# Rows of the batch-end store ordered by batch first instead of by token first

## Chip, cores and metric

The kernel runs on one core of a Trainium2 chip. The metric is device time in microseconds (us), the median of several executions. The span of a profile is some 1.8 us shorter than the time of the same execution.

## The reference

Attention with sliding-window masks (plain for four heads, dilated for four), then a mixture of experts with soft slots. Only the shape of the result matters here: 8 batches of 576 tokens give 4608 rows of 512 float32 numbers, 9.4 MB in all.

In outline (shortened, not the code itself):

```python
def reference(q, k, v, moe_phi, moe_w1, moe_w2):
    x = attention(q, k, v)                  # 8 batches x 576 tokens -> (4608, 512)
    logits = x @ phi                        # 32 slots
    slot_out = experts(softmax(logits, 0).T @ x, w1, w2)
    return softmax(logits, 1) @ slot_out    # (4608, 512), float32
```

## The kernel before

The last stage multiplies the exponentials of the logits (tile `o_et`, one column for each token) by the slot outputs, scales the rows while it evicts them from PSUM (the memory that takes TensorE's results), and stores them. It works in groups of 512 tokens: 128 partitions, each with four consecutive rows, so 8 KB that are contiguous in SBUF and in DRAM. 576 is not a multiple of 512. Groups 0 to 7 are the first 512 tokens of each batch; group 8 collects the last 64 tokens of all eight batches. Its exponentials are first copied together on GpSimd, and it is written by the batch-end store, whose 128 runs of 8 KB lie in eight places in DRAM, 576 rows apart.

```python
    def tok(G, j):                                  # weights of one output matmul
        return (a(o_et + 576 * G + j, [[4, 128]]) if G < 8 else
                a(o_tail + j, [[4, 128]]))
    # ... cut ...
    op(POOL, lambda: pool.tensor_copy(              # the tail copy
        a(o_tail, [[4, 8], [32, 16], [1, 4]]), a(o_et + 512, [[576, 8], [4, 16], [1, 4]])), ...)
    # ... cut ...
    def store(G, c0, cw, prio, j0=0, n=4):
        if G < 8:
            dst = out[576 * G:576 * G + 512, c0:c0 + cw].rearrange("(p j) f -> p j f", j=4)[:, j0:j0 + n, :]
            src = af(ostg(G) + 2 * (512 * j0 + c0), [[512, n], [1, cw]])
        else:                                       # the batch-end store: partition 8i+b
            dst = out.rearrange("(b r) f -> b r f", b=8)[:, 512:576, :].rearrange("b (i j) f -> i b (j f)", j=4)
            src = af(ostg(G), [[1, 2048]])
        store_ops.append(op(SP, lambda: spq.dma_start(dst, src), ...))
    # ... cut: ten stores of 256 KB, one of 512 KB, and then six of 1 MB, in this order:
    for G, x in [(2, 2)] + [(G, x) for G in (8, 3, 4, 5, 6, 7) for x in (0, 2)]:
```

The softmax here doesn't subtract the row's maximum and nothing guards it: scores larger than these inputs give would overflow.

## Time and profile before

| | before |
|---|---|
| time, median | 180.82 us |
| span of the profile | 179.0 us |
| last instruction of a compute engine ends | 164.5 us |
| rest of the span, stores draining | 14.5 us |

The chain of waits of before, its last pieces. The columns are start, length, and what.

```profile
120.53 32.06 DMA ar<-in_moe_w_dram
...
153.89 8.63 DVE ar L913 x15
...
163.18 1.32 DVE ar L913 x2
```

Up to 152.6 us the kernel waits for expert weights, then it evicts output tiles (L913) until 163.18 + 1.32 = 164.5 us. The chain as the profile follows it stops there. What runs on to 179.0 us is seen in the stretches. Here the columns are the stretch and its length, busy time of each engine (PE is TensorE, PEld its weight loads, DVE VectorE, ACT ScalarE, POOL GpSimd; SP, below, is the engine that issues the stores), the granted TensorE clock, the mean busy share of the 16 DMA engines, and GB/s. A packet counts whole in the stretch in which it starts, so a share can pass 1.

```profile
core 0: us, PE busy (x) PEld busy (x) DVE busy (x) ACT busy (x) POOL busy (x), PEclk, DMA share, GB/s
159.00:161.00 2.00, 1.93 (x9) 0.44 (x6) 2.00 (x4) 2.00 (x5) 0.00 (x0) 1.00 1.10 373
161.00:163.00 2.00, 1.26 (x5) 0.26 (x3) 2.00 (x4) 2.00 (x4) 0.00 (x0) 1.00 0.96 205
163.00:165.00 2.00, 0.00 (x0) 0.00 (x0) 1.50 (x3) 0.22 (x1) 0.00 (x0) 1.00 1.07 307
165.00:167.00 2.00, 0.00 (x0) 0.00 (x0) 0.00 (x0) 0.00 (x0) 0.00 (x0) 0.77 0.94 381
167.00:169.00 2.00, 0.00 (x0) 0.00 (x0) 0.00 (x0) 0.00 (x0) 0.00 (x0) 0.50 1.00 418
...
175.00:177.00 2.00, 0.00 (x0) 0.00 (x0) 0.00 (x0) 0.00 (x0) 0.00 (x0) 0.50 0.95 397
177.00:179.00 2.00, 0.00 (x0) 0.00 (x0) 0.00 (x0) 0.00 (x0) 0.00 (x0) 0.50 0.18 74
```

The DMA engines are busy without a break from before 160 us to 177 us (shares of 0.94 to 1.10): the end of the kernel is a queue of stores that drains. In the stretch from 161 to 163 us they are as busy as later (0.96 against 1.00 at 167 to 169 us) but move only half as much (205 against 418 GB/s). That is when the batch-end store runs. It was issued at 158.0 us and took 8.3 us to land, as the view of the output tensor, cut to that moment, shows:

```profile
L926 SPq DMA_DIRECT2D out_dram<-ar x1: 648/648/648, 158.0 to 158.0; - x1
...
DMA to landing us min/median/max: 8.3/8.3/8.3
```

The trace also keeps a record of every DMA packet (start, duration, bytes, queue; not the engine). Of the 768 packets of 8 KB that the six whole-tile stores make, the median takes 309 ns and 88 take more than 450 ns. Because one packet follows the other almost without a gap, packets can be strung together by their times; these are two such strings through the batch-end store of before, in ns:

```
795 596 631 558 518 645 386 606
309 572 598 818 309 309 309 684
```

### The profile page before, as it was taken

Reading aid. Unit: us, or ns where it says so; the run is one execution under the profiler, and the core shown is the slowest. Engines: PE = TensorE matmul, PEld = TensorE weight load, DVE = VectorE, ACT = ScalarE, POOL = GpSimd, SP = SyncE. Lnnn points to the kernel's source line nnn. Section 1 sums busy time; section 2 is a strip of 40 time slices with the busy share of each in tenths; the row PEclk is TensorE's granted clock in tenths of the full one; section 3 lists DMA queues with packets and bytes.
Section 4 is the critical chain, followed back from the end, with each engine's and each line's share of the span. In section 5 each row is a group of like instructions: output and inputs, shape, how many; then the busy total and the mean of one; then the engine's idle time right before and its main releaser. Section 6 shows DMA issues by size and latency. Waiting matters only on the chain.

```text
span 179.0 us, 4780 instructions
## 1 busy us (share of the span) xinstructions
PE 127.9 (71%) x2093; PEld 87.5 (49%) x2094; DVE 118.0 (66%) x220; ACT 104.7 (58%) x165; POOL 51.7 (29%) x103
## 2 busy tenths in 40 slices
PE   0009778989789989989699989976697657892000
PEld 0006556666567767767477767664444224420000
DVE  6898579788899899899589699383300015797000
ACT  2405299797789799798666889875111004694000
POOL 7559741332423432333930000790100000000000
PEclk9999999999999999999965999999879999999555
DMA  6999999999999999999999999999999999899996
GB/s 185 234 213 210 217 207 215 211 211 210 218 207 213 215 209 210 215 210 210 215 208 212 213 211 217 211 215 210 219 209 217 196 195 230 304 356 264 421 419 260
DMA packets 19220, 41.26 MB, mean 230 GB/s; under 512 B 1920, under 2 KB 8576, under 8 KB 18304
## 3 DMA queue, kind: packets, MB, share of 16 engines
q0 software_dynamic: 15056, 30.41, 90.0%
q1 hardware_dynamic: 4144, 10.55, 16.6%
q8 instruction: 16, 0.26, 0.5%
q14 instruction: 4, 0.03, 0.0%
HBM read 61.93 MB, written 9.44 MB: 399 GB/s over the span
## 4 chain that ended last, share of the span: by engine, by line
DMA 32%; PE 23%; DVE 23%; ACT 6%; POOL 4%; issue 2%; DVEq 0%
DMA ar<-in_moe_w_dram 18%; DMA ar<-in_k_dram 15%; PE ps L509 7%; DVE ar L488 6%; DVE ar L913 6%; ACT ar L548 4%; POOL ar L371 4%; PE ps L603 3%; DVE ar L614 3%; PE ps L570 3%; PE ps L516 2%; PE ps L526 2%; PE ps L693 2%; DVE ar L494 2%; DVE ar L445 2%
## 5 line engine op out<-in xcount | busy, mean ns | idle before, releaser
L548 ACT ACTIVATE ar<-ps 128x1152 bf16<-128x1152 f32 (+1 forms) x32 | 38.0, 1186 | 22.8 <-PE ps L533 12.5
L488 DVE STREAM_TRANSPOSE ar<-ar 128x576 uint32<-128x576 uint32 x40 | 48.4, 1240 | 3.1 <-DMA ar<-in_k_dram 2.9
L509 PE MATMUL ps<-ar 128*128 128x320 bf16 (+1 forms) x128 | 23.9, 313 | 15.4 <-DVE ar L488 13.1
L614 DVE TENSOR_TENSOR ar<-ps,fs 96x768 bf16<-96x768 f32 (+1 forms) x32 | 26.3, 823 | 1.2
L576 ACT ACTIVATE ar<-ps 128x768 bf16<-128x768 bf16 x32 | 24.8, 811 | 2.2 <-PE ps L570 2.2
L509 PEld LDWEIGHTS ps<-ar 128*128 128x128 bf16 x128 | 10.9, 102 | 20.1 <-POOL ar L418 13.1
L603 PE MATMUL ps<-ar 128*128 128x65 bf16 x320 | 15.7, 200 | 3.4 <-ACT ar L548 3.1
L570 PE MATMUL ps<-ar 128*128 128x128 bf16 x192 | 16.3, 232 | 2.2 <-DVE ar L614 1.9
L910 ACT ACTIVATE ar<-ps,fs 128x512 f32<-128x512 f32 (+1 forms) x23 | 11.4, 641 | 8.3 <-PE ps L901 8.3
L603 PEld LDWEIGHTS ps<-ar 128*128 128x128 bf16 x320 | 12.9, 101 | 6.3 <-ACT ar L548 3.8
L335 POOL DMA_DIRECT2D ar<-in_k_dram x16 | 8.9, 553 | 23.1 <-DVE ar L488 18.2
L610 DVE RECIPROCAL fs<-ps 96x12 f32<-96x12 f32 (+1 forms) x32 | 6.4, 200 | 12.6 <-PE ps L603 12.4
L570 PEld LDWEIGHTS ps<-ar 128*128 128x128 bf16 x192 | 12.8, 120 | 3.6 <-DVE ar L614 2.4
L857 PE MATMUL ps<-ar 128*32 128x512 bf16 (+1 forms) x80 | 10.5, 338 | 5.0 <-DMA ar<-in_moe_w_dram 3.5
L913 DVE TENSOR_SCALAR ar<-ps,fs 128x512 f32<-128x512 f32 (+1 forms) x23 | 12.7, 628 | 1.0 <-PE ps L901 1.0
L364 POOL DMA_DIRECT2D ar<-in_moe_w_dram x12 | 6.4, 580 | 22.2 <-DVE ar L488 22.2
L335 POOL DMA_DIRECT2D ar<-in_q_dram x16 | 8.7, 546 | 11.5 <-DVE fs L610 6.6
L335 POOL DMA_DIRECT2D ar<-in_v_dram x16 | 8.8, 549 | 9.2 <-DVE fs L610 5.5
L670 ACT ACTIVATE ar<-ps 128x576 bf16<-128x576 bf16 x16 | 9.6, 652 | 2.3 <-PE ps L654 2.3
L901 PE MATMUL ps<-ar 128*128 128x512 bf16 (+1 forms) x45 | 9.8, 339 | 1.5 <-DVE ar L881 1.0
L693 PE MATMUL ps<-ar 128*128 128x288 bf16 x64 | 9.2, 287 | 1.2 <-ACT ar L677 1.2
L857 PEld LDWEIGHTS ps<-ar 128*32 128x32 bf16 x80 | 4.7, 96 | 10.6 <-DMA ar<-in_moe_w_dram 6.8
(75 smaller groups left out, 192.6 us busy)
## 6 DMA issues: line engine op xcount, KB each, us to landing
ar<-in_moe_w_dram POOLq DMA_DIRECT2D x29, 512.0 KB, 27.2
out_dram<-ar SPq DMA_DIRECT2D x6, 1024.0 KB, 11.0
ar<-in_k_dram POOLq DMA_DIRECT2D x16, 288.0 KB, 21.8
ar<-in_q_dram POOLq DMA_DIRECT2D x16, 288.0 KB, 22.3
ar<-in_v_dram POOLq DMA_DIRECT2D x16, 288.0 KB, 22.3
out_dram<-ar SPq DMA_DIRECT2D x10, 256.0 KB, 3.8
ar<-in_moe_w_dram SPq DMA_DIRECT2D x1, 1024.0 KB, 4.9
ar<-in_moe_w_dram POOLq DMA_DIRECT2D x2, 256.0 KB, 31.7
```

What stands on the lines that cost most here:

```text
L335: return pool.dma_start(a(o_stg + (s * 3 + j) * 1152, [[1, 1152]]), src[b, 4 * dl:4 * dl + 4].rearrange("h (p t) d -> (h p) (t d)", p=32))
L488: return dve.transpose(au(o_dst, [[1, 18], [18, 32]]), au(src, [[32, 18], [1, 32]]))
L509: pe.matmul(pf(h, 0, [[1, W]]), a(o_id, [[1, 128]]), a(msk, [[1, W]]), start=True, stop=False)
L548: eo = op(ACT, lambda P=P, W=W: act.activation(a(P, [[W, 4], [1, W]]), AP(ps, 0, [[4096, 128], [512, 4], [1, W]]), ACTF.Exp, scale=SCALE), ...
L570: last = pe.transpose(pb(bank.idx, bb * 256 + par * 32, [[64, 4], [1, 32]]), src, a(o_id, [[1, 128]]))
L576: op(ACT, lambda t=t, bank=bank: act.activation(a(o_vb[vs] + 3 * t * VBK, [[66, 12], [2, 32], [1, 2]]), pb(bank.idx, 0, [[64, 12], [1, 32] ...
L603: last = pe.matmul(pf(bank.idx + x, 65 * t, [[1, 65]]), w, a(VB + t * VBK + 66 * h, [[1, 65]]), start=True, stop=True)
L614: op(DVE, lambda hp=hp, bank=bank: dve.tensor_tensor(a(ox + 128 * hp, [[64, 2], [256, NT], [1, 64]], 0, rows), pf(bank.idx, 0, [[512, 2], ...
L693: last = pe.matmul(pf(bank.idx, 0, [[1, 288]]), a(o_phis + 128 * c, [[1, 128]]), a(o_xt[xt] + 576 * c + 288 * g, [[1, 288]]), start=(c == ...
L857: last = pe.matmul(pf(sobank[x].idx, 0, [[1, n]], 32 * j, 32), a(o_htz + 1024 * g + 128 * c + 32 * j, [[1, 32]]), a(w2off(e) + DM * c + co ...
L910: op(ACT, lambda: act.activation(dst, src(), ACTF.Copy, scale=sca), actt(cw, .1), prio + .1, reads=[bank, b_rinv], writes=wr, name=f"OE{G} ...
L913: op(DVE, lambda: dve.tensor_scalar(dst, src(), sca, None, op0=AluOp.mult), dvet(cw, True) + .08, prio + .1, reads=[bank, b_rinv], writes= ...
```

## The change

The intent is to have the batch-end store write the 64 rows of one batch, 128 KB in one piece, from 16 neighbouring partitions, and to make the tail copy simpler. Partition 8i+b becomes partition 16b+i.

```diff
     op(POOL, lambda: pool.tensor_copy(
-        a(o_tail, [[4, 8], [32, 16], [1, 4]]), a(o_et + 512, [[576, 8], [4, 16], [1, 4]])), .8, T1 + 4, reads=[b_et],
+        a(o_tail, [[64, 8], [1, 64]]), a(o_et + 512, [[576, 8], [1, 64]])), .8, T1 + 4, reads=[b_et],
         writes=[b_tail], name="tail")
@@
-            dst = out.rearrange("(b r) f -> b r f", b=8)[:, 512:576, :].rearrange("b (i j) f -> i b (j f)", j=4)
+            dst = out.rearrange("(b r) f -> b r f", b=8)[:, 512:576, :].rearrange("b (i j) f -> b i (j f)", j=4)
```

The instruction lists of the two kernels differ in these two instructions only; the destination goes from 16x8x2048 to 8x16x2048.

## The prediction

> **What bounds the kernel now.** From 120.5 to 152.6 us the chain of waits sits on weight loads, then on output evictions (VectorE, 8.6 us). After 164.5 us no compute engine works any more; the span ends at 179.0 us: the last 14.5 us are the store queue draining. Between 167 and 177 us the DMA share is 0.95 to 1.04, at 397 to 438 GB/s (windows). The queue is behind from about 160 us on: the batch-end store is issued at 158.0 us and lands 8.3 us later, while the last of the five whole-tile stores behind it is issued at 166.1 us. So what a DMA engine loses in the batch-end store comes out at the end, one for one, on the slowest engine.
>
> **The batch-end store is already slow.** In the DMA records, 8 KB packets of the later stores take 309 ns; those of this store, between about 160.5 and 165.9 us, mostly take 550 to 650 ns (the stretch 161 to 163 us moved only 205 GB/s at 0.96 busy). [...] A rival reading is interference at the HBM end.
>
> **What the change does.** The GpSimd copy into the tail tile has the same 128x512 elements (630 ns, at 125.4 us, needed only after 152 us) and no other compute instruction changes: worth 0. The store keeps 128 runs of 8 KB, but its destination's outermost dimension goes from 16 to 8. [...] Eight engines then carry 16 packets each instead of 8, the others none; the later stores stay evenly split, so the loaded engines end last.
>
> **Cost (estimates from packet durations).** Before: eight packets at about 540 ns mean, slowest engine about 5.3 us. After: sixteen packets. Without collisions 16 x 0.309 = 4.9 us: no change. [...] 16 x 0.54 = 8.6 us: +3.3 us. [...] I expect nearly the worst of the three: 186.8 us (+3.3%), range 181.5 to 191. Chances: faster by over 2% 0.02, within 2% 0.25, slower by over 2% 0.73.
>
> **What would show it.** The store's issue to landing grows from 8.3 us to about 14 us; its packets stay at 600 to 900 ns; the drain after the last eviction grows from 14.5 to about 20 us; in the last 4 to 8 us only half of the DMA engines are busy (share near 0.5).
>
> **What would make it wrong.** If the store still spreads over 16 engines, there is no imbalance, and without collisions the time could fall by up to 2.6 us. If the present slowness comes from HBM and batch-first order cures it, doubling packets and halving their time cancel: no change. If engines drift out of step, collisions fade and the loss is 2 to 3 us, within 2%.

## The result, and the profile after

| | before | after |
|---|---|---|
| time, median | 180.85 us | 190.01 us |
| ratio, 95% interval | 1 | 1.0508 (1.0486 to 1.053) |
| span | 179.0 us | 188.0 us |
| last eviction ends | 164.5 us | 164.5 us |
| stores draining after it | 14.5 us | 23.5 us |

A ratio here is the mean time of one kernel's fast runs over that of the other's in the same rounds, so it is not quite the ratio of the medians quoted.

The evictions of after end where they did. This is the last piece of its chain of waits:

```profile
163.22 1.32 DVE ar L913 x2
```

So the whole 9 us is in the drain. Its stretches, same columns:

```profile
core 0: us, PE busy (x) PEld busy (x) DVE busy (x) ACT busy (x) POOL busy (x), PEclk, DMA share, GB/s
...
161.00:163.00 2.00, 1.30 (x5) 0.26 (x3) 2.00 (x4) 2.00 (x4) 0.00 (x0) 1.00 1.01 258
163.00:165.00 2.00, 0.00 (x0) 0.00 (x0) 1.53 (x3) 0.27 (x1) 0.00 (x0) 0.72 0.83 242
165.00:167.00 2.00, 0.00 (x0) 0.00 (x0) 0.00 (x0) 0.00 (x0) 0.00 (x0) 0.50 0.88 254
...
177.00:179.00 2.00, 0.00 (x0) 0.00 (x0) 0.00 (x0) 0.00 (x0) 0.00 (x0) 0.50 0.58 246
179.00:181.00 2.00, 0.00 (x0) 0.00 (x0) 0.00 (x0) 0.00 (x0) 0.00 (x0) 0.50 0.36 152
181.00:183.00 2.00, 0.00 (x0) 0.00 (x0) 0.00 (x0) 0.00 (x0) 0.00 (x0) 0.50 0.24 102
183.00:185.00 2.00, 0.00 (x0) 0.00 (x0) 0.00 (x0) 0.00 (x0) 0.00 (x0) 0.50 0.22 94
185.00:187.00 2.00, 0.00 (x0) 0.00 (x0) 0.00 (x0) 0.00 (x0) 0.00 (x0) 0.50 0.13 53
```

From 179 us on fewer and fewer engines work, and the last 2 us belong to 0.13 x 16 = 2 of them. An engine that works to 187 us with 40 packets of later stores (five stores, eight packets each) at 309 ns to do must have finished the batch-end store 12.4 us earlier, at about 174.6 us. This store's first packet starts at 160.5 us, so its 16 packets took about 14.1 us. This is worked out from the stretches and the packet times; the profile gives no landing time for this store. The records of 4 bytes, one from each engine at the end of each store, agree: on the two engines that end last they come 2.45 us apart, and the sixth from the end is at 174.73 and 174.92 us. So the store took these two engines 14.2 to 14.4 us, 0.89 to 0.90 us a packet on the mean.

One line of the page counts the packets of the SP queue, here of before and then of after:

```profile
q1 hardware_dynamic: 4144, 10.55, 16.6%
```

```profile
q1 hardware_dynamic: 4136, 10.55, 16.3%
```

The bytes are the same and eight packets are missing, all of 4 bytes in the records. In before there are 304 of them for the 19 transfers of this queue (17 stores and two loads), 16 to each, which fits one completion signal from each DMA engine that takes part. So the store uses eight engines now. In the records of after, 125 of the 768 packets of 8 KB take over 450 ns, and 29 take over 1000 ns (12 of them 1170 to 1190 ns, 3.8 times the 309 ns of a quiet packet); in before none takes over 1000.

The records of after show more when they are strung together. Of the eight engines that have nothing of the batch-end store, six do their first later store, eight packets, at 309 ns each and end it at 163.05 to 163.14 us. The two others take 594 to 613 ns for seven of their eight packets and end it at about 165.4 us. Four of the loaded engines take 1179 to 1184 ns for each packet that starts between 161.2 and 162.9 us, and the other four mostly about 0.6 us. Against the 309 ns of a quiet packet, then, six of the engines that have gone ahead lose nothing, two take about twice as long, and four loaded ones 3.8 times as long. What decides which is which is not in the profile: the records name neither engine nor partition, and the strings are put together by their times alone. The single execution of dst_only, below, shows the same first ends: six at 163.21 to 163.28 us, two at 165.53 and 165.68 us.

### The profile page after: what moved, and what is told of

Its sections match the earlier page's. It is cut to its first block, busy times and chain, and to the rows that moved or that the text cites. A ratio compares the mean times of both kernels' runs of the same rounds, so it can differ in the third digit from the quotient of the medians.

```text
span 188.0 us, 4781 instructions
## 1 busy us (share of the span) xinstructions
PE 125.3 (67%) x2094; PEld 84.9 (45%) x2094; DVE 117.2 (62%) x220; ACT 105.1 (56%) x165; POOL 51.7 (28%) x103
## 4 chain that ended last, share of the span: by engine, by line
DMA 57%; DVE 19%; PE 4%; POOL 4%; issue 2%; ACT 1%; DVEq 0%
DMA ar<-in_k_dram 39%; DMA ar<-in_moe_w_dram 18%; DVE ar L488 6%; DVE ar L913 5%; POOL ar L371 3%; DVE ar L614 2%; PE ps L509 1%; DVE ar L445 1%; DVE ar L450 1%; PE ps L570 1%; PE ps L516 1%; ACT ar L670 1%; ACT ar L548 1%; POOL ar L364 1%; DVE ar L494 1%
## 5 line engine op out<-in xcount | busy, mean ns | idle before, releaser
L509 PE MATMUL ps<-ar 128*128 128x320 bf16 (+1 forms) x128 | 22.8, 302 | 15.8 <-DVE ar L488 13.1
L509 PEld LDWEIGHTS ps<-ar 128*128 128x128 bf16 x128 | 10.5, 99 | 20.4 <-POOL ar L418 13.1
L603 PE MATMUL ps<-ar 128*128 128x65 bf16 x320 | 14.7, 193 | 3.3 <-ACT ar L548 3.2
L857 PE MATMUL ps<-ar 128*32 128x512 bf16 (+1 forms) x80 | 11.5, 367 | 5.7 <-DMA ar<-in_moe_w_dram 5.1
L570 PEld LDWEIGHTS ps<-ar 128*128 128x128 bf16 x192 | 12.4, 118 | 5.3 <-DVE ar L614 3.8
L603 PEld LDWEIGHTS ps<-ar 128*128 128x128 bf16 x320 | 12.0, 97 | 6.0 <-ACT ar L548 3.7
L901 PE MATMUL ps<-ar 128*128 128x512 bf16 (+1 forms) x46 | 10.8, 367 | 1.3 <-DVE ar L881 1.0
L857 PEld LDWEIGHTS ps<-ar 128*32 128x32 bf16 x80 | 5.3, 104 | 11.7 <-DMA ar<-in_moe_w_dram 8.0
```

The lines of the kernel that those rows point to most:

```text
L509: pe.matmul(pf(h, 0, [[1, W]]), a(o_id, [[1, 128]]), a(msk, [[1, W]]), start=True, stop=False)
L570: last = pe.transpose(pb(bank.idx, bb * 256 + par * 32, [[64, 4], [1, 32]]), src, a(o_id, [[1, 128]]))
L603: last = pe.matmul(pf(bank.idx + x, 65 * t, [[1, 65]]), w, a(VB + t * VBK + 66 * h, [[1, 65]]), start=True, stop=True)
L857: last = pe.matmul(pf(sobank[x].idx, 0, [[1, n]], 32 * j, 32), a(o_htz + 1024 * g + 128 * c + 32 * j, [[1, 32]]), a(w2off(e) + DM * c + co ...
```

## The experiments

Four theories stand against each other: the loss is **imbalance** (eight engines carry 16 packets each, and the rest of the queue is split evenly); it is **collisions within the store** (engines at work on it slow each other, depending on the SBUF partitions that they read); it is **meetings** (the loaded engines run into those that have gone ahead to the next stores); or it is **DRAM** (the order of addresses). Which partitions would collide was the author's assumption, and the layouts of per_batch and split4_last were chosen by it; the runs test it by packet times alone. The control per_batch_i and per_batch set collisions within the store against DRAM.

### dst_only: the store without the copy

```diff
 # before, with the new destination and the old tail copy
-    .rearrange("b (i j) f -> i b (j f)", j=4)
+    .rearrange("b (i j) f -> b i (j f)", j=4)
```

> Only the store's destination order of the change, with the old tail copy; rows are stored in the wrong place, so the result is wrong on purpose. If the whole loss is the store's, 190 us; what is missing from that is the copy's share, expected 0.

Measured: 189.58 us in one execution (before 180.92 us), its result wrong. The loss is the store's; the copy's share is at most some tenths.

### per_batch_i and per_batch: the same DRAM order from other partitions

```diff
 # batch-end store cut into eight, one for each batch bb
+            for bb in range(8):
+                d8 = out[576 * bb + 512:576 * bb + 576, :].rearrange("(i j) f -> i (j f)", j=4)
+                s8 = <16 partitions: bb, bb + 8, ... bb + 120>       # per_batch_i, with the copy of before
+                s8 = af(ostg(G), [[1, 2048]], 16 * bb, 16)           # per_batch, with the copy of after
```

> Before, with the batch-end store cut into eight stores of 16 rows of 8 KB, one for each batch; the row of each batch and block leaves from the same SBUF partition (8i+b) as before [...]. It is the control for the next run. Both theories [...] expect the same packets as before, 550 to 650 ns, and 180.8 to 182 us; the excess over 180.8 is the cost of issuing seven more stores.

> After, with the store cut into eight stores, one for each batch: 16 rows of 8 KB from the 16 neighbouring partitions 16b to 16b+15. DRAM addresses and their order by engine are the same as in the control; only the SBUF partitions differ, and all 16 engines carry eight packets again. [...] packets of about 1200 ns, the store takes about 9.9 us in place of 5.3, and the time is about 185 us, some 4.5 us over the control. DRAM theory: packets and time as in the control. Pure imbalance theory (the loss of the change comes only from eight engines carrying all): as in the control, since nothing is unbalanced.

Measured: per_batch_i 180.59 us (ratio 0.9988, 0.9973 to 1.0003), per_batch 181.46 us (1.0035, 1.0018 to 1.0053). In per_batch_i no packet takes over 788 ns; in per_batch 19 take over 1000 ns. Both send the same rows to the same DRAM addresses in the same eight stores, with 16 engines (4256 packets of the queue in both, 112 or 7 x 16 more than in before), so the long packets come with the other SBUF partitions: this speaks against DRAM. Which engine writes which row is not in the records. The expected 1200 ns and 4.5 us were the author's estimates of collisions within the store, for four engines that slow each other, which is not shown; the 4.5 us became 0.9 us. The records show why a packet's length is a poor measure of the loss (the mean over all 768 packets is 358 ns, against 342 in per_batch_i). Three strings of per_batch (ns):

```
1232 309 867 309 391
1160 309 1049 309 309
994 309 966 309 309
```

After a packet of 1.0 to 1.2 us comes one of 309 ns, so the store as a whole does not take four times as long; why is not shown. Issuing may pace this store too: the eight issues take 5.6 us on SP, about as long as the packets of this store in before (160.5 to 165.9 us). The run shows collisions, but is a poor measure of their price.

### after_last: eight engines, nobody ahead of them

```diff
-    for G, x in [(2, 2)] + [(G, x) for G in (8, 3, 4, 5, 6, 7) for x in (0, 2)]:
+    for G, x in [(2, 2)] + [(G, x) for G in (3, 4, 5, 6, 7, 8) for x in (0, 2)]:
```

> After, with the batch-end store issued last instead of first of the six whole-tile stores. The same eight engines carry 16 packets, but no later store runs beside them. If part of the 9 us comes from meeting the engines that have gone ahead [...], that part goes: [...] 16 packets at about 0.6 us = 9.6 us at the end, total about 185 us. If the loss comes from the engines' own collisions and imbalance alone, position does not matter and it stays at 190 us. In the last 8 to 10 us the DMA share should be 0.5 at some 105 GB/s.

Measured: 182.95 us (1.0116, 1.01 to 1.0133). Moving the store to the end wins back 7.1 us of the 9.2. Its last stretches:

```profile
173.00:175.00 2.00, 0.00 (x0) 0.00 (x0) 0.00 (x0) 0.00 (x0) 0.00 (x0) 0.50 0.59 127
175.00:177.00 2.00, 0.00 (x0) 0.00 (x0) 0.00 (x0) 0.00 (x0) 0.00 (x0) 0.50 0.43 123
177.00:179.00 2.00, 0.00 (x0) 0.00 (x0) 0.00 (x0) 0.00 (x0) 0.00 (x0) 0.50 0.48 188
179.00:181.00 2.00, 0.00 (x0) 0.00 (x0) 0.00 (x0) 0.00 (x0) 0.00 (x0) 0.50 0.21 90
```

Half of the engines work; at first they move 123 to 127 GB/s, then 188. A string of 16 packets says the same (ns):

```
606 629 631 565 562 625 474 316 567 321 312 312 309 309 309 309
```

Seven of the first nine packets take 562 to 631 ns, the last seven 309 to 321 ns: the collisions end within the store. That the engines start in step and then fall out of step is the author's reading and not shown. I had expected all 16 packets to stay near 0.6 us (9.6 us); the store took some 7 us (7.16 us in this string).

### split4_last: the same imbalance without collisions

The tail copy is laid out so that partition 32x+4b+i holds four rows of batch b, and the store is cut into four.

```diff
 # after_last, and:
+            for x in range(4):
+                d8 = out(batch, row, f)[:, 512 + 16 * x:528 + 16 * x, :].rearrange("b (i j) f -> b i (j f)", j=4)
+                s8 = af(ostg(G), [[1, 2048]], 32 * x, 32)          # 32 partitions for each part
```

> As after_last, but the last store is cut into four, each of 8 batches by 4 rows from 32 partitions, [...]. Still eight engines with 16 packets each, so the imbalance is that of after_last. [...] packets of 309 ns, 16 of them = 5 us at the end at some 210 GB/s, total about 180.5 us, 4 to 5 us under after_last. If collisions are not the cause, as after_last.

Measured: 180.93 us (1.0008, 0.9993 to 1.0023). The queue shows eight completion packets for each of the four stores (4160 packets in all, 16 more than before), so there are eight engines here too.

```profile
173.00:175.00 2.00, 0.00 (x0) 0.00 (x0) 0.00 (x0) 0.00 (x0) 0.00 (x0) 0.50 0.48 197
175.00:177.00 2.00, 0.00 (x0) 0.00 (x0) 0.00 (x0) 0.00 (x0) 0.00 (x0) 0.50 0.54 197
177.00:179.00 2.00, 0.00 (x0) 0.00 (x0) 0.00 (x0) 0.00 (x0) 0.00 (x0) 0.50 0.23 98
```

Half of the engines (shares of 0.48 and 0.54) move almost half of the full rate (197 GB/s against 426 at 171 to 173 us). Only 8 packets of 768 take over 450 ns, none over 596: this layout hardly collides, as the author had assumed. The imbalance is that of after_last, the place in the queue too, and the time is 2.0 us shorter: that is the price of collisions within the store. It also speaks against DRAM again, as each part is still stored by batch first.

### split4_here: the same four parts at the old place

```diff
 # split4_last, with the order of before
-    ... (3, 4, 5, 6, 7, 8) ...
+    ... (8, 3, 4, 5, 6, 7) ...
```

> The four-part batch-end store of split4_last, at its old place, ahead of the five other whole-tile stores. Eight engines carry it, they never meet one another; [...] If meeting engines that have gone ahead is what costs, this is 8 packets at 309 ns and 8 at about 618, 7.4 us, 2.5 us over split4_last: about 183 us. If imbalance alone costs nothing and meetings cost nothing, 181 us. If the place in the queue itself costs [...], near the 190 us of after.

That half of the packets would meet an engine that has gone ahead, and take twice 309 ns then, was the author's estimate; no run shows it.

Measured: 181.72 us (1.0049, 1.0032 to 1.0065), 0.8 us over split4_last where 2.5 were expected. The profile shows that the run tested less than it was to test:

```profile
161.00:163.00 2.00, 1.47 (x5) 0.26 (x3) 2.00 (x4) 2.00 (x5) 0.00 (x0) 1.00 0.50 197
163.00:165.00 2.00, 0.00 (x0) 0.00 (x0) 1.71 (x3) 0.43 (x1) 0.00 (x0) 1.00 0.72 242
165.00:167.00 2.00, 0.00 (x0) 0.00 (x0) 0.00 (x0) 0.00 (x0) 0.00 (x0) 1.00 0.94 225
```

Issuing four parts took SP until 162.45 us, and the next store had not reached the other eight engines before about 164.3 us: until then they were idle, and nobody was met. From 165 to 167 us, when both kinds are at work, 0.94 of the engines move only 225 GB/s. The place in the queue alone does not cost 9 us; the size of the meetings is left to the next run.

### after_hold: a wait added

```diff
 # after, with one dependency more
+                            after=[<the batch-end store>]   # stores behind it are issued when it has landed
```

> After, with one wait added: the store behind the batch-end store is issued only when that store has landed, so nothing runs beside its eight engines, and eight engines stand idle meanwhile. All stores, their order and their addresses are those of after. If the loss of after comes from the loaded engines meeting those that have gone ahead [...], the batch-end store now takes some 7 us, as in after_last, and with a gap of about 2 us for landing and issuing the total is about 185 us: a wait that saves some 5 us. If the meetings are not what costs, the wait can only add: 190 us or more.

Measured: 184.58 us (1.0202, 1.0187 to 1.0217). All stores, addresses and their order are those of after; SP waits 9.3 us for the store to land, eight engines are idle meanwhile, and the kernel is 5.4 us faster than after.

```profile
161.00:163.00 2.00, 1.46 (x5) 0.26 (x3) 2.00 (x4) 2.00 (x5) 0.00 (x0) 1.00 0.49 98
163.00:165.00 2.00, 0.00 (x0) 0.00 (x0) 1.70 (x3) 0.43 (x1) 0.00 (x0) 1.00 0.48 147
165.00:167.00 2.00, 0.00 (x0) 0.00 (x0) 0.00 (x0) 0.00 (x0) 0.00 (x0) 0.80 0.50 193
167.00:169.00 2.00, 0.00 (x0) 0.00 (x0) 0.00 (x0) 0.00 (x0) 0.00 (x0) 0.50 0.13 53
169.00:171.00 2.00, 0.00 (x0) 0.00 (x0) 0.00 (x0) 0.00 (x0) 0.00 (x0) 0.50 0.96 393
```

The share of 0.48 to 0.50 while this store is alone is a second sign of eight engines. No packet takes over 845 ns: the packets of 1.2 us of after came only with another store beside. The gap (0.13 at 167 to 169 us) is the price of the wait; it is the likely cause of the 1.6 us by which this run is slower than after_last, but no run separates it.

### before_last: the same move with 16 engines

```diff
 # before, with the order of after_last
-    ... (8, 3, 4, 5, 6, 7) ...
+    ... (3, 4, 5, 6, 7, 8) ...
```

> Before, with its 16-engine batch-end store issued last. Here all engines carry it at once in either place, so few meet engines that have gone ahead: 180 to 181 us, within 0.5% of before, against the 7 us that the same move was worth with eight engines (190.0 to 182.95 us). If the place in the queue itself costs, some us faster than before.

Measured: 180.13 us (0.9958, 0.9945 to 0.9971). With 16 engines the place is worth 0.4%, with eight it was worth 7.1 us.

### uniform and uniform2: no batch-end store at all

Group G takes rows 512G to 512G+511 regardless of batches. All stores are then even runs of 128 rows of 8 KB, and the tail copy goes. In uniform all row sums come from one block of 36 small matmuls at the end; in uniform2 they come with the sums of each batch.

```diff
-        return (a(o_et + 576 * G + j, [[4, 128]]) if G < 8 else a(o_tail + j, [[4, 128]]))
+        return a(o_et + 512 * G + j, [[4, 128]])
@@ store
-        dst = out[576 * G:576 * G + 512, ...   (and the batch-end case)
+        dst = out[512 * G:512 * G + 512, c0:c0 + cw].rearrange("(p j) f -> p j f", j=4)[:, j0:j0 + n, :]
@@ uniform2, in the matmuls of the sums of batch b (batch 7 also for group 8)
+            for t in range(4 * b, 4 * b + (8 if b == 7 else 4)):
+                last = pe.matmul(pf(bank.idx, 363 + t - 4 * b, [[1, 1]]), tok(t // 4, t % 4), a(o_rm, [[1, 1]]), ...)
```

> Before, with the nine output groups laid over the 4608 rows without regard to batches (group G holds rows 512G to 512G+511, the row sums and their reciprocals are taken for all groups at once in the idle time before the last weights come), so that every whole-tile store is one even run of 128 rows of 8 KB and there is no batch-end store and no tail copy. If the batch-end store of before loses some 2.6 us [...], all six stores run at 309 ns a packet from about 160.5 us on and the time is about 178.2 us (1.5% under before). If its slow packets cost nothing because something else paces the drain, it stays at 180.8.

Measured: 180.40 us (0.9975, 0.9952 to 0.9998), correct. The drain was as hoped, but it began later. The pieces of its chain of waits before the drain, and the same piece of before:

```profile
146.81 4.51 PE ps L849 x55
...
155.17 0.44 DVE ar L873
...
156.11 8.64 DVE ar L905 x15
```

```profile
152.95 0.44 DVE ar L881
```

The last sum of slot outputs (L873, L881 in before) ends 2.2 us later, in the slowest of six executions (179.85 to 181.25 us), which is the one profiled. TensorE was behind: its first block of expert matmuls begins at 139.83 us (L810), in before at 129.22 us (L818). I read this as the kernel's own scheduler, with the small operations gone, ordering the attention stage otherwise. One change had become two. The second version keeps the order of instructions.

> The even groups of 512 rows again, but now with the row sums taken batch by batch, in the same matmul group and PSUM bank as the sums of before (four more one-column matmuls for each batch), so that the order of instructions on every engine is that of before; in uniform it had shifted, and the first output evictions began 4 us later than in before. Expected: the drain begins as in before, all six whole-tile stores run at 309 ns a packet, and the time is 178.2 to 179.3 us (0.9 to 1.5% under before). If the even store does not help, 180.8.

Measured: 178.49 us (0.9863, 0.9846 to 0.988), correct. It beats both kernels.

```profile
159.00:161.00 2.00, 1.93 (x8) 0.55 (x7) 2.00 (x4) 2.00 (x5) 0.00 (x0) 1.00 1.08 423
161.00:163.00 2.00, 1.45 (x5) 0.26 (x3) 2.00 (x4) 2.00 (x5) 0.00 (x0) 1.00 1.02 418
163.00:165.00 2.00, 0.00 (x0) 0.00 (x0) 1.69 (x3) 0.42 (x1) 0.00 (x0) 1.00 0.98 406
...
175.00:177.00 2.00, 0.00 (x0) 0.00 (x0) 0.00 (x0) 0.00 (x0) 0.00 (x0) 0.50 0.32 131
```

The hole of 205 GB/s at 161 us is gone (418 now), and no packet of 8 KB takes over 342 ns.

## Why the prediction was right or wrong

The runs can be put in a row, from no disturbance to all of them. The price of a row is the difference of its ratio to the row above, taken of 180.85 us.

| run | engines of the store | collisions within | meetings | ratio to before | price |
|---|---|---|---|---|---|
| uniform2 | 16 | no | no | 0.9863 | |
| split4_last | 8 | no | no | 1.0008 | 2.6 us |
| after_last | 8 | yes | no | 1.0116 | 2.0 us |
| after | 8 | yes | yes | 1.0508 | 7.1 us |

Before itself stands 2.5 us over uniform2, with 16 engines and collisions. So the net loss of 9.2 us is 2.6 us of imbalance less the 2.5 us of collisions that before had, then 2.0 us of collisions among the eight engines, then 7.1 us of meetings. The rows differ in a few other things (four stores in place of one in split4_last, no copy in uniform2), so a few tenths of these prices are not settled. "Meetings" stands for all that another store beside this one costs. What they meet at is not shown: the packets over 1000 ns are gone in after_hold, but holding stores back also keeps the queue of stores short, and no run separates the two. The strings of after speak against a queue that is too long and against a busy DRAM: either would have to spare exactly the six engines that kept 309 ns beside the loaded ones.

- *The number, 186.8 us.* Measured were 190.01 us, inside the range of 181.5 to 191 but near its end: a loss of 9.2 us in place of 6.0. Collisions within the store were put at 3.3 us (2.1 measured, below). The other 2.7 us were an estimate for the meetings that rested on no measured packet time (7.1 measured). The two were off in opposite directions; that these errors partly cancel is luck.
- *What bounds the end.* Right: evictions end at 164.5 us in both kernels, and all of the change is in the drain.
- *The copy is worth nothing.* Right within the noise of one execution (dst_only 189.58 us).
- *Eight engines instead of sixteen.* Right, and now shown: eight completion packets fewer, and a share of 0.48 to 0.50 while the store runs alone in after_hold. No run had shown it when it was predicted.
- *The slow packets come from the SBUF side, not from DRAM.* Right as far as the runs go: with the same DRAM order, other partitions gave 19 packets over 1000 ns (per_batch), and the layout of split4_last packets of 309 ns, with 8 of 768 over 450. Which engine read which partition is not in the profile.
- *"Without collisions 16 x 0.309 = 4.9 us: no change."* Right: split4_last, 1.0008.
- *"16 x 0.54 = 8.6 us: +3.3 us."* Too much. After_last costs 2.1 us over before, and its string is back at 309 to 321 ns after nine packets. The prediction had named this case: "If engines drift out of step, collisions fade and the loss is 2 to 3 us". The loss came out so only with the store at the end of the queue, where no other store runs beside it; that the engines drift out of step is not shown.
- *The meetings.* This is the term that was off, and too small: the slowest engine's packets took 0.89 us on the mean, 14.2 us in all, and the loss was 9.2 us. Twelve packets (1170 to 1190 ns) are as long as 3.8 quiet ones of 309 ns; four loaded engines took 1179 to 1184 ns where two that had gone ahead took 594 to 613 ns. Why they lose so unevenly is not shown.
- *"Only half of the engines busy in the last 4 to 8 us."* Only in part. The share was 0.58 at 177 to 179 us, but in the last 8 us it fell from 0.36 to 0.13: the eight loaded engines did not suffer alike, and the last two set the time.
- *Issue to landing of 14 us* could not be read, as the profile gives no landing for this store after the change. By the records of 4 bytes its last engine ends at 174.92 us, some 17 us after the issue at 158.1 us, so 14 was too low. *Packets of 600 to 900 ns* was wrong in its upper end (up to 1387 ns).

## What to carry to other kernels

Look at the outermost dimension of a store's access pattern: here 16 gave 16 DMA engines and 8 gave eight (16 and 8 completion packets), so an order that looked more contiguous halved them. With the runs of 8 KB unchanged, no run here gained from contiguity. In the queue that drains at the end of this kernel, a store on half of the engines did more than unbalance them: those that had nothing of it went ahead and got in the way of those that had, which cost most of the loss (7.1 of 9.2 us), and a wait that held them back made the kernel faster (by 5.4 us). What paid was to regroup the rows so that every store is one even pattern over all 128 partitions (uniform2, 1.4% under before), with the order of the other instructions kept (uniform, without it, gained 0.25%).
